# Hash attention and a quick-GELU feed-forward in fp32: the softmax divisors of a pair's two query halves in one TensorE step on four column quarters

## The chip, the cores and the metric

The kernel runs on one core of a Trainium2 chip. The metric is the device time of one launch in microseconds (us), as the median of several runs.

## What is computed

An attention block is followed by a feed-forward block, all in float32. Two positions may attend to each other only if the signs of six projections agree; a row sum of exponentials then divides each attention row.

```python
q_bits = (np.einsum('bhsd,dk->bhsk', q, proj) > 0).astype(np.int64)   # k_bits alike
mask = q_bucket[:, :, :, None] == k_bucket[:, :, None, :]
scores = np.where(mask, scale * np.matmul(q, k.transpose(0, 1, 3, 2)), -1000000000.0)
attn = np.exp(scores - np.max(scores, axis=-1, keepdims=True))
attn = attn / (np.sum(attn, axis=-1, keepdims=True) + 1e-09)
x = np.matmul(attn, v)                     # then (B, H, S, D) -> (B*S, H*D)
h = x @ w_in
g = h * (1.0 / (1.0 + np.exp(-1.702 * h)))
out = g @ w_out
```

B = 4, H = 8, S = 768, D = 64, so x is 3072 x 512; w_in is 512 x 2048 and w_out 2048 x 512, both handed over as 64-bit floats.

## The kernel before, in words

The heads are taken two at a time: 16 pairs, `pairs[n]`, with the two heads of a pair on partitions 0 to 63 and 64 to 127. The 768 queries of a pair are done in two halves of 384 columns (`HS`), c = 0 and c = 1. The loop at L525 runs over `groups`, which are these halves (those of pair 0 are each cut in two again), and hands out the work of group g together with what is left of the group before it, `prev`. The order of the instructions on TensorE (PE), VectorE (DVE), ScalarE (ACT) and GpSimd (POOL) is the order in which this Python code issues them (`manual_schedule`); the engines run side by side and wait for each other by semaphores. SyncE (SP) holds the DMA queue, in order too.

One group does the following.

- `scores` (L429): for each of six tiles of 128 keys, both heads, first a product of hash features in bf16 and then one of keys and queries in float32, into a PSUM tile `ps` (three buffers). ACT takes the exponential of each into `e` (L430); there is one `e` for c = 0 and one for c = 1.
- `add_low` on POOL (L437, L438) sums the exponentials of key tiles 0 to 2 into `acc0` (one buffer).
- `add_high` on DVE (L443, L445), for `prev`: sums key tiles 3 to 5 and `acc0` into `acc` (one buffer).
- `total` (L472), for `prev`: one matmul per head with a 128 x 64 block of ones. It sums `acc` over the 128 partitions and puts the sum on all 64 partitions of the head: `dn`, in PSUM, in a buffer that the hash products share (tag "m", one buffer).
- `invert` (L479, L481): DVE transposes `dn` in 32 x 32 blocks, so that of each block only one column is needed, and takes the reciprocals of 12 values per partition. In the next group `spread` (L486) transposes them back, broadcast over 32, and `norm` (L490) multiplies the attention output in `xT` by them.
- `values` (L453), for `prev`: the product of `e` and v into `av`; `unload` (L465, L466) on ACT takes it to `xT`.
- In a c = 0 group DVE turns k and q of the next pair (L388), ACT measures them (L395), and TensorE makes their hash products (`hashed`, L405); in the c = 1 group after it `featured` (L410) turns these into features on DVE, which DMAs (L417) spread to `kf` and `qf`.

In between, pairs 1 to 14 convert one chunk of w_in each from 64 to 32 bits (`convert`, L158). After the DMA into `raw` (L162) come six steps on DVE: L175, L179, L183, L190, L192, L195; with the third, ACT squares the high words into `size` (L187), which L195 reads. L575 issues `4 - c` steps per group: four in the c = 0 group, the last two in the c = 1 group. L579 then starts the next chunk's DMA, on SP's queue. In the last four pairs the c = 0 group also issues one of the sums `x_sums` (L577) for the feed-forward block.

After the pairs comes the feed-forward block: products L699 with w_in, the activation, products L812 with w_out, whose details the change does not touch. The last pair's second `total` is issued after the first part of it.

Of the kernel before, what the change touches and what calls it, by code (L numbers as in the profile page):

```python
# [8 lines left out]
F32 = mybir.dt.float32  # L9
BF16 = mybir.dt.bfloat16  # L10
I32 = mybir.dt.int32
U32 = mybir.dt.uint32
Act = mybir.ActivationFunctionType
Alu = mybir.AluOpType
# [5 lines left out]
P = 128  # L20
# [18 lines left out]
def kernel(  # L39
# [17 lines left out]
    nc = tc.nc  # L57

    loader = [nc.sync]
    B, H, S, D = q.shape  # L60
# [3 lines left out]
    T = S // P  # L64
# [3 lines left out]
    HS = HT * P  # L68
# [10 lines left out]
    ones = const.tile([P, D], F32, name="ones")  # L79
# [30 lines left out]
    for i, x in enumerate("kq"):  # L110
# [7 lines left out]
        for c in range(2):  # L118
            r0 = D * i + 32 * c
# [29 lines left out]
    CW = 512  # L149
# [3 lines left out]
    for x in (0x3FFFFFFF, 0xFF800000):  # L153
        m = const.tile([P, 1], U32, name=f"mask_{x:x}")
# [3 lines left out]
    def convert(cv, dst, src, queue=None, psum=None):  # L158


        raw = cv.tile([P, CW, 2], U32, tag="raw", name="raw")
        (queue or loader[0]).dma_start(out=raw, in_=src)  # L162

        def of(x):
            return x if len(dst.shape) == 2 else x.rearrange("p (x r) -> p x r", r=dst.shape[2])

        lo, hi = raw[:, :, 0], raw[:, :, 1]
        bits = cv.tile([P, CW], U32, tag="bits", name="bits")
        part = (cv if psum is None else psum).tile([P, CW], U32, tag="part", name="part")
        size = (cv if psum is None else psum).tile([P, CW], F32, tag="size", name="size")  # L170
        yield


        if psum is None:
            nc.vector.scalar_tensor_tensor(part, hi, 3, masks[0x3FFFFFFF], op0=Alu.logical_shift_left, op1=Alu.bitwise_and)  # L175
        else:
            nc.vector.tensor_scalar(part, hi, 3, 0x3FFFFFFF, op0=Alu.logical_shift_left, op1=Alu.bitwise_and)
        yield
        nc.vector.scalar_tensor_tensor(bits, hi, 0xC0000000, part, op0=Alu.bitwise_and, op1=Alu.bitwise_or)  # L179
        yield  # L180

        if psum is None:
            nc.vector.tensor_tensor(part, bits, masks[0xFF800000], op=Alu.bitwise_and)  # L183
        else:
            nc.vector.tensor_scalar(part, bits, 0xFF800000, None, op0=Alu.bitwise_and)

        nc.scalar.activation(size, hi.bitcast(F32), Act.Square)  # L187
        part = part.bitcast(F32)
        yield
        nc.vector.scalar_tensor_tensor(part, lo, 2.0**-52, part, op0=Alu.mult, op1=Alu.mult)  # L190
        yield
        nc.vector.tensor_tensor(dst, of(bits.bitcast(F32)), of(part), op=Alu.add)  # L192
        yield

        nc.vector.scalar_tensor_tensor(dst, of(size), (1.125 * 2.0**-15) ** 2, dst, op0=Alu.is_ge, op1=Alu.mult)  # L195
# [84 lines left out]
    def attention(ff):  # L280


        GT = T // 2
        actx = ExitStack()
        with actx:
            ld = actx.enter_context(tc.tile_pool(name="ld", bufs=1))
            wk = actx.enter_context(tc.tile_pool(name="wk", bufs=2))
            cv = actx.enter_context(tc.tile_pool(name="cv", bufs=1))
            st = actx.enter_context(tc.tile_pool(name="st", bufs=2))
            aps = actx.enter_context(tc.tile_pool(name="aps", bufs=1, space=PSUM))  # L290
            mps = actx.enter_context(tc.tile_pool(name="mps", bufs=1, space=PSUM))
# [140 lines left out]
            accs, avs = {}, {}  # L432
# [6 lines left out]

            def add_high(n, c):  # L440
                e = [es[c][:, GT + i, :, 0:HS] for i in range(GT)]
                acc = accs[n, c] = st.tile([P, 2, HS], F32, tag="acc", name="acc", bufs=1)
                nc.vector.scalar_tensor_tensor(acc, e[0], T * TINY, e[1], op0=Alu.add, op1=Alu.add)  # L443
                for x in (e[2], accs.pop((n, c, 0))):
                    nc.vector.tensor_tensor(acc, acc, x, op=Alu.add)  # L445
# [7 lines left out]
                        nc.tensor.matmul(av[D * j : D * (j + 1), :], vt[:, t, j, :], es[c][:, t, j, :],  # L453
                                         start=(t == 0), stop=(t == T - 1))

            def x_of(n, c):
                b, hp = pairs[n]
                x = xT[:, hp, b * S : (b + 1) * S]
                x = x.rearrange("d (t p) -> d t p", p=P) if n else x.rearrange("d (p t) -> d t p", p=P)
                return x[:, c * GT : (c + 1) * GT, :]  # L460

            def unload(n, c):
                av = avs.pop((n, c))
                vs = st.tile([P, 1], F32, tag="vs", name="vs")
                nc.scalar.copy(vs, av[:, HS : HS + 1])  # L465
                nc.scalar.activation(x_of(n, c), av[:, 0:HS].rearrange("p (t s) -> p t s", t=GT), Act.Identity, bias=vs[:, 0:1])  # L466

            def total(n, c):
                acc = accs.pop((n, c))
                dn = accs[n, c] = mps.tile([P, HS], F32, tag="m", name="dn")  # L470
                for j in range(2):
                    nc.tensor.matmul(dn[D * j : D * (j + 1), :], ones, acc[:, j, :], start=True, stop=True)  # L472

            def invert(n, c):


                dn = accs.pop((n, c))
                rt = st.tile([P, HS], F32, tag="rt", name="rt")
                nc.vector.transpose(rt, dn)  # L479
                r = st.tile([P, HS // 32, 1], F32, tag="r", name="r")  # L480
                nc.vector.reciprocal(r, rt.rearrange("p (s i) -> p s i", i=32)[:, :, 0:1])  # L481
                accs[n, c] = rt, r

            def spread(n, c):
                rt, r = accs[n, c]
                nc.vector.transpose(rt.rearrange("p (s i) -> p s i", i=32), r.to_broadcast([P, HS // 32, 32]))  # L486

            def norm(n, c):
                rt, r = accs.pop((n, c))
                nc.vector.tensor_tensor(x_of(n, c), x_of(n, c), rt.rearrange("p (t s) -> p t s", t=GT), op=Alu.mult)  # L490


            groups = [(n, c, kts) for n in range(len(pairs)) for c in range(2)
# [4 lines left out]
            def step(n, count=1):  # L498
                for _ in range(count):
                    next(conv.get(n, iter(())), None)  # L500
# [19 lines left out]
            totals, norms, hashes = [], [], []  # L520
# [4 lines left out]
            for g in range(len(groups) + 2):  # L525
                n, c, kts = groups[g] if g < len(groups) else (last + 1, 0, ())
                prev = groups[g - 1] if 1 <= g <= len(groups) else None
                if kts:
                    scores(n, c, kts)
                    if g == 0:  # L530
                        rest()
                    if kts[0] == 0:
                        add_low(n, c)


                if hashes:
                    featured(hashes.pop())
                ended = prev and prev[2][-1] == T - 1
                if ended:
                    add_high(*prev[:2])  # L540
                    totals.append((g + (g == len(groups) or len(kts) == GT), prev[:2]))
                for x in norms:
                    spread(*x)

                turned = ("", "k", "q", "")[g] if n == 0 else "kq" if c == 0 and n < last else ""
                for x in turned:
                    turn(n + 1, x)
                    measure(n + 1, x)
                if c == 1 or n == 0:
                    while norms:  # L550
                        norm(*norms.pop(0))
                inverted = []
                while totals and totals[0][0] == g:
                    inverted.append(totals.pop(0)[1])
                    total(*inverted[-1])
                    invert(*inverted[-1])
                while norms:
                    norm(*norms.pop(0))
                norms += inverted
                if prev:  # L560
                    values(*prev)
                if ended:
                    unload(*prev[:2])
                if "q" in turned:
                    hashed(n + 1)
                    if n:
                        hashes.append(n + 1)
                    else:
                        featured(n + 1)
                    for x in "kq":  # L570
                        if n + 2 <= last:
                            fetch(n + 2, x)
                    fetch_v(n + 1)
                if kts and kts[-1] == T - 1:
                    step(n, 4 - c)  # L575
                    if c == 0 and n > last - len(x_sums):
                        x_sums[n - last - 1]()  # L577
                    if c == 1:
                        begin(n + 1)  # L579
                if g == len(groups) - 1:  # L580
                    guard(0)
                if g == len(groups):
                    guard(1)
                    for f in in_sums(0):
                        f()
                    early.close()
                    next(ff)
            for x in norms:
                spread(*x)
                norm(*x)  # L590


    def shifted_attention():
# [405 lines left out]
```

## Time and profile before

| | us |
|---|---|
| median of 3 runs | 890.97 (890.84 to 891.78) |
| the profiled execution: its own time | 890.56 |
| its span, first to last instruction | 888.7 |
| attention, up to the first product of the feed-forward block | about 334 |
| one pair in the steady part of it | 20.04 |

How to read it. The span is what the profile sees of the profiled execution; the remaining 1.9 us of its own time lie outside of it. The page gives for each engine the busy time, then the chain of work that ended last: followed back from the last instruction, at each step to what released it. A timeline row has the start and the length in us, the engine, the line, the operation, what it writes and reads, and in brackets an idle time ahead of it with what ended it. `dn<-acc,ones` at L472 is `total`. A float32 matmul leaves two records in the trace: the 32 steps of `total`, two matmuls each, are 128 records.

The groups that the change touches, from the page and the answers on lines (mean ns of one):

| line | engine, what | count | mean ns |
|---|---|---|---|
| L472 | PE `dn<-acc,ones`, 128*64, 384 columns | 128 records | 512 |
| L405 | PE `hash<-kT,pf_k` and `hash<-qT,pf_q`, 128*32, 384 columns | 120 records | 498 |
| L479 | DVE transpose `rt<-dn` 128x384 | 32 | 580 |
| L481 | DVE reciprocal `r<-rt` 128x12 | 32 | 229 |
| L486 | DVE transpose `rt<-r` 128x384 | 32 | 572 |
| L490 | DVE product `xT<-xT,rt` 128x384 | 32 | 1020 (493 to 1816) |
| L187 | ACT square `size<-raw` 128x512 | 32 (16 of w_in) | 648 |
| L195 | DVE last conversion step, w_in 128x512 | 16 | 692 |

### The profile page before, as it was taken

Reading aid. Unit: us, or ns where it says so; the run is one execution under the profiler, and the core shown is the slowest. Engines: PE = TensorE matmul, PEld = TensorE weight load, DVE = VectorE, ACT = ScalarE, POOL = GpSimd, SP = SyncE. Lnnn points to the kernel's source line nnn. Section 1 sums busy time; section 2 is a strip of 40 time slices with the busy share of each in tenths; the row PEclk is TensorE's granted clock in tenths of the full one; section 3 lists DMA queues with packets and bytes.
Section 4 is the critical chain, followed back from the end, with each engine's and each line's share of the span. In section 5 each row is a group of like instructions: output and inputs, shape, how many; then the busy total and the mean of one; then the engine's idle time right before and its main releaser. Section 6 shows DMA issues by size and latency. Waiting matters only on the chain.

```text
span 888.7 us, 11969 instructions
## 1 busy us (share of the span) xinstructions
PE 873.2 (98%) x4077; PEld 503.5 (57%) x4077; DVE 709.3 (80%) x1020; ACT 313.9 (35%) x519; POOL 309.7 (35%) x275
## 2 busy tenths in 40 slices
PE   9899999999999999999999999999999999999995
PEld 4444444444444444444444444444888888888884
DVE  4698887888889964777788787888798977897785
ACT  5755666666665642233222223322100000000000
POOL 4243233222333263666434435559932000000000
PEclk9999999999999999999999999999999999999998
DMA  4745544556544103555455545565845665467524
GB/s 103 122 83 84 103 81 81 86 98 96 97 83 82 46 1 107 188 191 189 177 209 194 201 155 202 189 236 194 301 156 190 190 210 216 159 220 237 190 96 97
DMA packets 169477, 132.01 MB, mean 149 GB/s; under 512 B 123936, under 2 KB 138432, under 8 KB 164032
## 3 DMA queue, kind: packets, MB, share of 16 engines
q1 hardware_dynamic: 167712, 129.69, 51.0%
q10 hardware_dynamic: 1696, 1.48, 0.6%
q8 instruction: 34, 0.56, 0.3%
q14 instruction: 35, 0.29, 0.1%
HBM read 79.69 MB, written 50.33 MB: 146 GB/s over the span
## 4 chain that ended last, share of the span: by engine, by line
PE 96%; DVE 2%; DMA 1%; ACTq 0%; issue 0%; SPq 0%; ACT 0%; DVEq 0%
PE product L699 32%; PE product L812 28%; PE ps L429 16%; PE av L453 14%; PE dn L472 3%; PE hash L405 1%; DMA q<-in_q_dram 1%; PE tp L363 0%; ACTq L417 0%; DVE xT L816 0%; PE warm L356 0%; PE hash L370 0%; DVE y L791 0%; DVE acc L445 0%; SPq L325 0%
## 5 line engine op out<-in xcount | busy, mean ns | idle before, releaser
L430 ACT ACTIVATE e<-ps 128x768 f32<-128x768 f32 x192 | 151.5, 813 | 19.3 <-PE ps L429 13.4
L429 PE MATMUL ps<-qT,kT 64*128 64x384 f32 x768 | 155.1, 482 | 0.0
L699 PE MATMUL product<-xT,w_in_sb 128*128 128x512 f32 x288 | 135.4, 592 | 0.0
L453 PE MATMUL av<-e,v 128*64 128x385 f32 x768 | 130.2, 486 | 0.9 <-ACT xT L466 0.9
L437 POOL TENSOR_TENSOR acc<-e 128x768 f32<-128x768 f32 x32 | 49.6, 1551 | 208.1 <-ACT e L430 103.3
L707 ACT ACTIVATE c<-c 128x512 f32<-128x512 f32 x72 | 45.5, 632 | 186.2 <-issue 78.8
L453 PEld LDWEIGHTS av<-e,v 128*64 128x64 f32 x768 | 54.9, 136 | 70.5 <-issue 69.0
L699 PEld LDWEIGHTS product<-xT,w_in_sb 128*128 128x128 f32 x288 | 54.6, 190 | 68.5 <-issue 63.4
L699 PE MATMUL product<-t_x,s_in 128*128 128x512 f32 x192 | 90.2, 592 | 0.0
L429 PEld LDWEIGHTS ps<-qT,kT 64*128 64x128 f32 x768 | 68.2, 188 | 35.5 <-issue 35.5
L216 POOL TENSOR_TENSOR v<-c,u 128x512 f32<-128x512 f32 x24 | 34.3, 1427 | 129.2 <-ACT c L707 129.2
L818 ACT COPY u<-product 128x256 f32<-128x256 f32 x21 | 7.8, 373 | 167.7 <-PE product L812 125.6
L429 PE MATMUL ps<-qf,kf 64*128 64x384 bf16 x384 | 63.0, 324 | 0.7 <-ACT e L430 0.5
L699 PEld LDWEIGHTS product<-t_x,s_in 128*128 128x128 f32 x192 | 36.5, 190 | 45.9 <-issue 43.8
L438 POOL TENSOR_TENSOR acc<-acc,e 128x768 f32<-128x768 f32 x32 | 56.7, 1772 | 2.5
L699 PE MATMUL product<-xT,s_in 128*128 128x512 f32 x96 | 45.1, 592 | 0.0
L699 PE MATMUL product<-t_x,w_in_sb 128*128 128x512 f32 x96 | 45.1, 592 | 0.0
L429 PEld LDWEIGHTS <-kf 64*128 64x128 bf16 x384 | 18.9, 94 | 42.2 <-issue 20.7
L479 DVE STREAM_TRANSPOSE rt<-dn 128x384 f32<-128x384 f32 x32 | 18.6, 580 | 25.7 <-PE dn L472 25.6
L465 ACT COPY vs<-av 128x1 f32<-128x1 f32 x32 | 5.1, 160 | 95.0 <-PE av L453 94.9
L812 PE MATMUL product<-raw_g,xT 128*128 128x256 f32 x152 | 35.1, 379 | 0.0
L490 DVE TENSOR_TENSOR xT<-xT,rt 128x384 f32<-128x384 f32 x32 | 32.6, 1020 | 1.7
(201 smaller groups left out, 1558.3 us busy)
## 6 DMA issues: line engine op xcount, KB each, us to landing
raw_g<-g_dram SPq DMA_DIRECT2D x22, 1024.0 KB
s_in<-g_dram SPq DMA_DIRECT2D x20, 1024.0 KB
g_dram<-c SPq DMA_DIRECT2D x72, 256.0 KB
g_dram<-t SPq DMA_DIRECT2D x48, 256.0 KB
raw<-in_moe_w_out_dram SPq DMA_DIRECT2D x16, 512.0 KB
raw<-in_moe_w_in_dram SPq DMA_DIRECT2D x15, 512.0 KB
v<-in_v_dram SPq DMA_DIRECT2D x32, 192.0 KB
g_dram<-u SPq DMA_DIRECT2D x24, 256.0 KB
```

The source lines that it names most:

```text
L216: return [lambda: eng.tensor_tensor(t1, b12, b11, op=Alu.subtract), lambda: eng.tensor_tensor(b12, b22, b12, op=Alu.subtract), lambda: eng ...
L429: nc.tensor.matmul(ps[:, j, 0:HS], a[hs, keys], m[hs, cols], start=not last, stop=last)
L430: nc.scalar.activation(es[c][:, kt, :, 0:HS], ps[:, :, 0:HS], Act.Exp, scale=1.0 / D**0.5)
L437: nc.gpsimd.tensor_tensor(acc, es[c][:, 0, :, 0:HS], es[c][:, 1, :, 0:HS], op=Alu.add)
L438: nc.gpsimd.tensor_tensor(acc, acc, es[c][:, 2, :, 0:HS], op=Alu.add)
L453: nc.tensor.matmul(av[D * j : D * (j + 1), :], vt[:, t, j, :], es[c][:, t, j, :], start=(t == 0), stop=(t == T - 1))
L472: nc.tensor.matmul(dn[D * j : D * (j + 1), :], ones, acc[:, j, :], start=True, stop=True)
L479: nc.vector.transpose(rt, dn)
L490: nc.vector.tensor_tensor(x_of(n, c), x_of(n, c), rt.rearrange("p (t s) -> p t s", t=GT), op=Alu.mult)
L699: nc.tensor.matmul(ps, wq[LEFT[i]][:, kc, :], xq[RIGHT[i]][:, kc, :], start=(kc == 0), stop=(kc == K2 - 1))
L707: nc.scalar.activation(c, c, Act.Gelu_apprx_sigmoid)
L812: nc.tensor.matmul(ps, wq[LEFT[i]][:, c, :], gq[RIGHT[i]][:, c, :], start=(c == 0), stop=(c == F4 - 1))
```

## The change

`total` now runs once per pair, after the sums of both halves are there: four matmuls with a 128 x 32 block of ones, each onto 32 partitions of `dn` (head j, half c on partitions 64 j + 32 c). `acc` has two buffers for it. `invert` transposes `dn` once; a reciprocal of 24 values per partition (the 12 values twice) fills `r`, and four small reciprocals, one for each strip of 32 partitions, put in what belongs to the other half: they read one strip and write another. One transpose of 768 columns spreads them, in the same group. `norm` multiplies 768 columns at once, in the group after. `rt` and the spread `rs` have one buffer each.

The conversion of w_in gives up the tiles `part` and `size`: `part` is made in the destination, and the square overwrites the high words in `raw`. `step` gets `2 + 2 * c`: two steps in the c = 0 group, four in the c = 1 group. In the order of the built program the changed instructions stand so: in a c = 0 group DVE has the sums of the c = 1 half before, turned k and q, `rt`, five reciprocals, the spread, two conversion steps; in a c = 1 group the features, the sums, the norm, four conversion steps. On ACT the square stands behind the unload of the c = 1 group, ahead of the exponentials of the next pair.

```diff
-        part = (cv if psum is None else psum).tile([P, CW], U32, tag="part", name="part")
-        size = (cv if psum is None else psum).tile([P, CW], F32, tag="size", name="size")
+        if psum is None:
+            part, size = dst.bitcast(U32), hi.bitcast(F32)
+        else:
+            part = psum.tile([P, CW], U32, tag="part", name="part")
+            size = psum.tile([P, CW], F32, tag="size", name="size")
...
-                acc = accs[n, c] = st.tile([P, 2, HS], F32, tag="acc", name="acc", bufs=1)
+                acc = accs[n, c] = st.tile([P, 2, HS], F32, tag="acc", name="acc")
...
-            def total(n, c):
-                acc = accs.pop((n, c))
-                dn = accs[n, c] = mps.tile([P, HS], F32, tag="m", name="dn")
-                for j in range(2):
-                    nc.tensor.matmul(dn[D * j : D * (j + 1), :], ones, acc[:, j, :], start=True, stop=True)
+            def total(n):
+                dn = accs[n] = mps.tile([P, HS], F32, tag="m", name="dn")
+                for c in range(2):
+                    acc = accs.pop((n, c))
+                    for j in range(2):
+                        r0 = D * j + 32 * c
+                        nc.tensor.matmul(dn[r0 : r0 + 32, :], ones[:, 0:32], acc[:, j, :], start=True, stop=True)
...
+            def invert(n):
+                dn = accs.pop(n)
+                rt = st.tile([P, HS // 32, 32], F32, tag="rt", name="rt", bufs=1)
+                nc.vector.transpose(rt.rearrange("p s i -> p (s i)"), dn)
+                r = st.tile([P, 2, HS // 32], F32, tag="r", name="r")
+                nc.vector.reciprocal(r, rt[:, :, 0].unsqueeze(1).to_broadcast([P, 2, HS // 32]))
+                for r0 in range(0, P, 32):
+                    c = r0 // 32 % 2
+                    r1 = r0 + 32 - 64 * c
+                    nc.vector.reciprocal(r[r1 : r1 + 32, c], rt[r0 : r0 + 32, :, 0])
+                rs = accs[n] = st.tile([P, S], F32, tag="rs", name="rs", bufs=1)
+                nc.vector.transpose(rs.rearrange("p (s i) -> p s i", i=32),
+                                    r.rearrange("p c s -> p (c s)").unsqueeze(2).to_broadcast([P, S // 32, 32]))
+
+            def norm(n):
+                x, rs = x_of(n), accs.pop(n)
+                nc.vector.tensor_tensor(x, x, rs.rearrange("p (t s) -> p t s", t=T), op=Alu.mult)
...
-                    totals.append((g + (g == len(groups) or len(kts) == GT), prev[:2]))
-                for x in norms:
-                    spread(*x)
+                    if prev[1] == 1:
+                        totals.append((g + (g == len(groups)), prev[0]))
...
                 while norms:
-                    norm(*norms.pop(0))
-                norms += inverted
+                    norm(norms.pop(0))
+                if totals and totals[0][0] == g:
+                    norms.append(totals.pop(0)[1])
+                    total(norms[-1])
+                    invert(norms[-1])
...
-                    step(n, 4 - c)
+                    step(n, 2 + 2 * c)
```

More of the change, by code (lines that the diff above doesn't have):

```diff
@@ L454, in values, with x_of @@
                                          start=(t == 0), stop=(t == T - 1))
-            def x_of(n, c):
+            def x_of(n):
                 b, hp = pairs[n]
                 x = xT[:, hp, b * S : (b + 1) * S]
-                x = x.rearrange("d (t p) -> d t p", p=P) if n else x.rearrange("d (p t) -> d t p", p=P)
-                return x[:, c * GT : (c + 1) * GT, :]
+                return x.rearrange("d (t p) -> d t p", p=P) if n else x.rearrange("d (p t) -> d t p", p=P)
             def unload(n, c):
@@ L465, in unload @@
                 nc.scalar.copy(vs, av[:, HS : HS + 1])
-                nc.scalar.activation(x_of(n, c), av[:, 0:HS].rearrange("p (t s) -> p t s", t=GT), Act.Identity, bias=vs[:, 0:1])
-            def total(n, c):
-                acc = accs.pop((n, c))
-                dn = accs[n, c] = mps.tile([P, HS], F32, tag="m", name="dn")
-                for j in range(2):
[L472 to L490, printed above, removed]
+                nc.scalar.activation(x_of(n)[:, c * GT : (c + 1) * GT, :], av[:, 0:HS].rearrange("p (t s) -> p t s", t=GT), Act.Identity, bias=vs[:, 0:1])
@@ L548, in attention @@
                     measure(n + 1, x)
-                if c == 1 or n == 0:
-                    while norms:
-                        norm(*norms.pop(0))
[L552 to L556, printed above, removed]
-                while norms:
-                    norm(*norms.pop(0))
-                norms += inverted
+                while norms:
+                    norm(norms.pop(0))
[3 more added lines that the diff above has]
+                    invert(norms[-1])
                 if prev:
@@ L588, in attention @@
             for x in norms:
-                spread(*x)
-                norm(*x)
+                norm(x)
     def shifted_attention():
```

## The prediction, made before the changed kernel was run

> **What bounds the kernel now.** I read the busy shares, then the chain that ended last in order of time, then each engine's timeline over one steady pair of heads.
>
> ```profile
> PE 873.2 (98%) x4077; PEld 503.5 (57%) x4077; DVE 709.3 (80%) x1020; ACT 313.9 (35%) x519; POOL 309.7 (35%) x275
> ```
>
> TensorE is nearly always busy. The chain over one steady pair (start us, us, what):
>
> ```profile
> 199.07 0.78 PE hash L405 x8
> 199.85 4.95 PE ps L429 x36
> 204.81 0.80 PE dn L472 x4
> 205.60 3.88 PE av L453 x24
> 209.48 4.95 PE ps L429 x36
> 214.44 0.80 PE dn L472 x4
> 215.23 3.88 PE av L453 x24
> ```
>
> The chain is TensorE alone, without gaps: 2 x (4.95 + 0.80 + 3.88) + 0.78 = 20.04 us per pair. Each step (half of the queries) pays 0.80 for `dn`. The hash, whose four outputs are 32 partitions each, does 8 records in 0.78; `dn` does 4 in 0.80.
>
> The timelines say what stands behind it (start us, us, engine, line):
>
> ```profile
> 207.88 0.69 DVE L195 SCALAR_TENSOR_TENSOR w_in_sb<-size,w_in_sb 128x512 f32<-128x512 f32 x1
> 208.50 0.95 DVE L443 SCALAR_TENSOR_TENSOR acc<-e 128x768 f32<-128x768 f32 x1
> 209.55 0.96 DVE L445 TENSOR_TENSOR acc<-acc,e 128x768 f32<-128x768 f32 x1
> 210.61 0.96 DVE L445 TENSOR_TENSOR acc<-acc,acc 128x768 f32<-128x768 f32 x1
> ...
> 215.28 0.58 DVE L479 STREAM_TRANSPOSE rt<-dn 128x384 f32<-128x384 f32 x1 [1.50 <-PE dn L472]
> ...
> 219.35 0.58 ACT L466 ACTIVATE xT<-av,vs 128x384 f32<-128x384 f32 x1
> 219.83 0.66 ACT L187 ACTIVATE size<-raw 128x512 f32<-128x512 f32 x1
> ...
> 224.23 1.51 DVE L490 TENSOR_TENSOR xT<-xT,rt 128x384 f32<-128x384 f32 x1
> 236.09 0.50 DVE L490 TENSOR_TENSOR xT<-xT,rt 128x384 f32<-128x384 f32 x1
> ```
>
> The sums `acc` are complete at 211.57, while TensorE asks for them only at 214.37: 2.8 us of slack. DVE is busy 17.10 us of 20.05 (stage table), so it is the next engine in line.
>
> **What the Trainium skill says.** "TensorE: Matmul & The Clock Gate", Part 3 on packing: matmuls whose outputs lie in different strips of 32 partitions run side by side. The hash agrees: four starts within 0.02 us (219.04 to 219.06). "TensorEngine Tiling (Array Packing)", Key Properties: a change of tiling mode drains TensorE. No cost shows: `av` takes 3.88 before a hash and before scores alike. "SBUF — State Buffer", Who interferes with whom: a VectorE instruction with two SBUF inputs and a GpSimd instruction exclude each other. The trace agrees: L490 took 1.51 while L437 ran on POOL, 0.50 without. "VectorE: DVE Perf Modes", Two Vector instructions with no wait between them: an instruction that starts in another quadrant than the one before is held until that has finished; this concerns the four small reciprocals, and no row of before shows it.
>
> **The change, part by part** (t counts from the start of a pair's first scores, 209.42 in these timelines).
>
> *TensorE.* Before 32 x 0.80 = 25.6 us; after, 16 steps of four quarters at the hash's 0.78 = 12.5. Bounds for the new step: 0.78, or 1.6 if quarters ran two by two; the hash has the same 128x32 weights and 384 columns, so I take 0.78. That is 0.82 per pair, 13.1 gross.
>
> *Start.* Pairs 0 and 1 don't get it. Without pair 0's first `dn` (25.68) the next scores still wait until 29.03, for ACT, which issues DMAs from 24.05 to 27.9. Without pair 1's first `dn` (44.39, 1.51 idle before it) TensorE runs ahead to 46.7, but the DVE is behind: it starts at 35.58, when q has landed, and has qT 0.98, rt 0.54, reciprocals 1.3, spread 0.9, two conversion steps 1.3, f 0.6, three sums 3.1, norm 1.0, three conversion steps 2.0 and some 2 to 3 us of POOL's lock ahead of L198 (L195 before), then 3.1 of sums: about 53.7, so pair 1's `dn` is at about 53.7 against 54.02. I take a gain of 0.3 (0 to 0.9). There remain 14 x 0.82 = 11.5.
>
> *The conversion's place.* Four, then two steps become two, then four; and `size` now lies in `raw`. On ACT the square L190 (L187 before) thus stands behind the second step's unload, just ahead of the next pair's exponentials; on DVE the last conversion step waits for it and stands ahead of L446/L448, the sums that the joint `dn` needs. This is the added wait. From the rows: vs at t = 0.11, unload at 0.30, square 0.48 later at 0.78, done at 1.44 (0.66); conversion step at 1.49, the next instruction 0.62 later at 2.11; the three sums as before 1.05 + 1.06 + 0.96, done at 5.18; TensorE at 5.23. It asks at 4.95. So 0.28; I take 0.30 (0 to 0.6). The first half's two matmuls do not wait and fill part of it. It affects the pairs 3 to 15 that follow a conversion, 13 x 0.30 = 3.9. The exponentials start about 0.38 later (1.46 for 1.10). The fourth scores tile, at 2.42, needs the first at 2.3: covered by 0.1; uncovered it costs that excess per pair.
>
> *DVE's chain.* Does it reach that step before the square has? From 1.49: step 0.62, sums 3.0, turns 1.72, rt 0.62; one reciprocal of 24 elements (12 take 0.23; 0.23 to 0.46, I take 0.33) and four of 12 (held: 0.23 each, range 0.14 to 0.45) with two waits 1.35; spread at the price of L388 0.94, next after 0.87; two conversion steps 1.32: t = 10.95. Hash's feature 0.60, sums 3.0, norm 0.96 (as L445; before two of 0.50 to 1.51): 15.5. Then three conversion steps with two SBUF inputs, 1.9 us, against POOL's pair 1.54 + 1.68, which starts when the sums free `acc0`: all serial, 20.8. The square is done at 19.5 + 1.44 = 21.0, the period being 20.04 - 0.80 - 0.02 + 0.30 = 19.5. So DVE is in time by 0.2 us: thin. In pairs 12 to 14 the x sums (issued at L577; 1.22 each, row L218) make it late by 0.9 at most, less where DVE takes the lock first; I take 0.5, 3 x 0.5 = 1.5.
>
> *Edits costed at nothing.* The unload is unchanged. Writing `part` into the destination moves no work. `raw` is free only when the last step has ended (t = 2.1), so its DMA, issued at -1.2 before, goes at about 2.2; the next issues behind it on SP wait for turned k anyway (216.15, t = 6.7). The DMA activity of before ends some 3 us after its issue, so it lands near 5.5, needed at 9.6: cover 4 us, and beyond it each us is on DVE's chain. The feature DMAs follow the k, q and v fetches on SP as before; the scores that need them come 0.8 earlier, and the four that the first tile needs were issued 3.8 us before it. The last pair's `dn` lies in the feed-forward stage in both. The square's strided write is unshown; I take 0.66, double would add 0.6 to each stall.
>
> *Sum.* 11.5 + 0.3 - 3.9 - 1.5 = 6.4 us. The profiled execution took 890.56 (span 888.7): 884.2. The median of the runs is 0.41 above it: 890.97 - 6.4 = **884.6**.
>
> **Rivals.** *B, no stall*: the square or the sums come a little earlier than summed, or TensorE's queue covers 0.28. For: 0.28 is small beside my roundings. Against: every term is a row. 11.5 + 0.9 gained: 878.6. *C, DVE binds without losing all*: small reciprocals near 0.35 or a worse order of the lock bring its chain to about 19.9. For: 0.2 us of cover. Gain 10 x 0.14 + 0.3, less 3 x (1.1 - 0.14) for the x sums: about -1, 892 at worst, 889 where the x sums find room; I set 890.3. *D, slower*: the same engine past the old period. Place: the serial stretch of reciprocals, spread and conversion ahead of the sums. It decides where the chain passes 20.04, 0.8 above my sum, as with held reciprocals of 0.45 together with a lock lost once more per pair: at 20.4, 13 x 0.36 + 3 x 1.1 - 0.3 = 7.7 lost, 898.7. Against: DVE does less in sum (two transposes of 0.58, two spreads of 0.57, two norms before). *E, the quarters don't run side by side*: `dn` stays at 1.6 per pair, and the wait lies under its first half; no gain, 890.9. Against: the hash.
>
> **Chances.** A, the forecast, 0.54 (own range 882 to 887.5); B 0.17; C 0.15; D 0.10; E 0.04. A measurement can tell about 0.2%, 1.8 us, from no change: 889.2 to 892.8 is the same. Faster: A, B and a third of C, 0.76; the same: E and the rest of C, 0.14; slower: D, 0.10. The range 879 to 890 takes in A, most of B and the better half of C.
>
> **What would show it.** Right: 16 groups of `dn`, 128x32, each about 0.78 in the chain; one period near 19.5; a short TensorE idle (about 0.3) ahead of `dn` released by the sums; DVE idle before the last conversion step, released by the square. B: no idle there, period 19.2. C and D: no DVE idle anywhere in the pair, TensorE idle before `dn` of 0.7 or more. Wrong altogether: `dn` near 1.6, or DVE waiting for `raw`.

## The result and the profile after

| | before | changed |
|---|---|---|
| median, six runs of each | 891.15 us | 887.89 us (886.93 to 889.4) |
| profiled execution: own time, span | 890.56, 888.7 | 887.43, 885.6 |

The ratio is 0.9965, with a 95% interval of 0.9952 to 0.9977: 3.3 us faster, where 6.4 were forecast. The time lies in the stated range of 879 to 890, but just above the forecast's own 882 to 887.5, and the gain is half of the forecast. The page after begins:

```profile
PE 869.4 (98%) x4077; PEld 501.0 (57%) x4077; DVE 723.3 (82%) x1020; ACT 309.2 (35%) x519; POOL 320.7 (36%) x275
```

TensorE still sets the time. The chain of the changed kernel over one steady pair (start us, us, what):

```profile
212.53 0.96 PE dn L477 x8
213.50 4.03 PE av L456 x24
217.53 0.78 PE hash L408 x8
218.31 4.95 PE ps L432 x36
223.26 4.03 PE av L456 x24
227.30 4.95 PE ps L432 x36
232.25 0.96 PE dn L477 x8
```

A pair now takes 232.25 - 212.53 = 19.72 us for 20.04 before. One `dn` of 0.80 is gone. The other one is eight records and takes 0.96, and both `av` take 4.03 where they took 3.88. This last difference was in no step of the prediction.

The wait that the change added, around one pair's end: VectorE first, then ScalarE. L190 is the square, L198 the last conversion step, L446 and L448 the sums.

```profile
203.12 2.03 DVE L186 TENSOR_TENSOR w_in_sb<-bits,mask_ff 128x512 uint32<-128x512 uint32 x1
205.19 2.05 DVE L193 SCALAR_TENSOR_TENSOR w_in_sb<-raw,w_in_sb 128x512 f32<-128x512 uint32 x1
207.27 0.69 DVE L195 TENSOR_TENSOR w_in_sb<-bits,w_in_sb 128x512 f32<-128x512 f32 x1
208.99 0.69 DVE L198 SCALAR_TENSOR_TENSOR w_in_sb<-raw,w_in_sb 128x512 f32<-128x512 f32 x1 [1.02 <-ACT raw L190]
...
211.65 0.96 DVE L448 TENSOR_TENSOR acc<-acc,acc 128x768 f32<-128x768 f32 x1
```

```profile
207.82 0.58 ACT L468 ACTIVATE xT<-av,vs 128x384 f32<-128x384 f32 x1
208.30 0.66 ACT L190 ACTIVATE raw<-raw 128x512 f32<-128x512 f32 x1
```

The last conversion step waits 1.02 us for the square, which ends at 208.96. The sums follow it and end at 212.61. The scores of this pair began at 207.52 in the timeline, so that is t = 5.09 where the prediction said 5.18, against a TensorE that asks at 4.95.

Where the 3.1 us of the two profiled spans came from, by landmarks of the two chains:

| stretch | before | changed | gain |
|---|---|---|---|
| start to pair 1's hash (22.44, 23.39) | 22.44 | 23.39 | -0.95 |
| to pair 3's hash (58.77, 59.78) | 36.33 | 36.39 | -0.06 |
| twelve pairs, to pair 15's hash (299.29, 296.73) | 240.52 | 236.95 | 3.57 |
| to `row`, the end of attention (333.94, 330.57) | 34.65 | 33.84 | 0.81 |
| feed-forward, to the end of the span | 554.76 | 555.03 | -0.27 |

The attention from the first hash on gained 4.32 us. The first stretch is the same code in both; in the profiles of the six kernels below it ended between 23.16 and 24.38, so the 22.44 of the kernel before is a quick start of that one execution and not an effect of the change.

### The profile page after: what moved, and what is told of

Its sections match the earlier page's. It is cut to its first block, busy times and chain, and to the rows that moved or that the text cites. A ratio compares the mean times of both kernels' runs of the same rounds, so it can differ in the third digit from the quotient of the medians.

```text
span 885.6 us, 11940 instructions
## 1 busy us (share of the span) xinstructions
PE 869.4 (98%) x4077; PEld 501.0 (57%) x4077; DVE 723.3 (82%) x1020; ACT 309.2 (35%) x519; POOL 320.7 (36%) x275
## 4 chain that ended last, share of the span: by engine, by line
PE 96%; DVE 2%; ACTq 0%; ACT 0%; issue 0%; DVEq 0%
PE product L699 33%; PE product L812 28%; PE ps L432 17%; PE av L456 14%; PE dn L477 2%; PE hash L408 1%; PE tp L366 1%; DVE acc L448 0%; ACTq L420 0%; DVE xT L816 0%; PE warm L359 0%; PE hash L373 0%; DVE y L791 0%; DVE w_in_sb L193 0%; DVE w_in_sb L186 0%
## 5 line engine op out<-in xcount | busy, mean ns | idle before, releaser
L433 ACT ACTIVATE e<-ps 128x768 f32<-128x768 f32 x192 | 148.4, 811 | 23.5 <-PE ps L432 18.3
L440 POOL TENSOR_TENSOR acc<-e 128x768 f32<-128x768 f32 x32 | 58.7, 1833 | 195.4 <-DVE acc L448 185.9
L456 PEld LDWEIGHTS av<-e,v 128*64 128x64 f32 x768 | 52.1, 136 | 77.6 <-issue 75.5
L441 POOL TENSOR_TENSOR acc<-acc,e 128x768 f32<-128x768 f32 x32 | 59.1, 1847 | 2.5
L446 DVE SCALAR_TENSOR_TENSOR acc<-e 128x768 f32<-128x768 f32 x32 | 30.5, 953 | 7.7 <-ACT e L433 7.7
L448 DVE TENSOR_TENSOR acc<-acc,e 128x768 f32<-128x768 f32 x32 | 32.0, 999 | 2.4
```

Of the source, the lines that this page charges most:

```text
L433: nc.scalar.activation(es[c][:, kt, :, 0:HS], ps[:, :, 0:HS], Act.Exp, scale=1.0 / D**0.5)
L440: nc.gpsimd.tensor_tensor(acc, es[c][:, 0, :, 0:HS], es[c][:, 1, :, 0:HS], op=Alu.add)
L441: nc.gpsimd.tensor_tensor(acc, acc, es[c][:, 2, :, 0:HS], op=Alu.add)
```

## The experiments

The *tiling* of a group of matmuls is what the trace's rows give as `64*128`, `128*64` or `128*32`: the shape of the block of weights that one of its float32 matmuls uses. Here the scores are 64x128, the values 128x64, the hash 128x32; the total was 128x64 before and is 128x32 now. Each experiment compares with the kernel before, run again beside it.

Theory 1, made from the two chains: a group of matmuls that follows one of another tiling pays an *entry* of about 0.15 us. The 0.80 of the old `dn` contained this entry. With `dn` gone, `av` stands behind the scores and pays it; and the new `dn`, on quarters, makes `av` pay it in the other step too. It can be seen in the weight loads (PEld). In the kernel before, after the 128x64 `dn`:

```profile
204.73 0.20 PEld L472 LDWEIGHTS dn<-acc,ones 128*64 128x64 f32 x4 [0.55 <-issue]
205.11 0.14 PEld L453 LDWEIGHTS av<-e,v 128*64 128x64 f32 x2 [0.18 <-issue]
```

`av` starts at 205.43 there: its first weights are loaded 0.32 us ahead, beside `dn`. In the changed kernel, after the 128x32 `dn`:

```profile
212.46 0.34 PEld L477 LDWEIGHTS dn<-acc,ones 128*32 128x32 f32 x8 [0.55 <-issue]
213.43 0.20 PEld L456 LDWEIGHTS av<-e,v 128*64 128x64 f32 x4 [0.62 <-issue]
```

`av` starts at 213.43, with its first load: nothing is loaded ahead. The rival, theory 2: `av` is slower for a reason of its own, or four quarters cost by their number of records.

**Only the tiling.** The kernel before, with each total on quarters:

```diff
-                    nc.tensor.matmul(dn[D * j : D * (j + 1), :], ones, acc[:, j, :], start=True, stop=True)
+                    for r0 in (D * j, D * j + 32):
+                        nc.tensor.matmul(dn[r0 : r0 + 32, :], ones[:, 0:32], acc[:, j, :], start=True, stop=True)
```

> The kernel before, with each of its 32 totals written as four 128x32 matmuls (each head's sum onto its two strips of 32 partitions) instead of two 128x64; same sums, everything else alike. Theory 1 (a change of TensorE's column tiling costs about 0.10 at the gap and 0.05 at the first step of the group that follows, because the weights can't be loaded ahead): dn and av are now in different tilings, so 0.15 more per total, a pair takes 20.34 instead of 20.04, about 4.8 us more in all: 896. Theory 2 (av is slower in the changed kernel for another reason, such as what its values or its buffer wait for; four quarters cost no more than two halves): a pair stays at 20.04, 891.

Measured: 896.78 us for 891.31 of the kernel before, ratio 1.006 (95% interval 1.0043 to 1.0076). Its chain:

```profile
203.75 4.95 PE ps L429 x36
208.70 0.78 PE dn L473 x8
209.48 4.03 PE av L453 x24
```

`dn` itself is no slower, 0.78. `av` goes from 3.88 to 4.03 although nothing about it was edited; a pair takes 20.32. Theory 1's price holds, and theory 2's first half falls. From pair 3's hash to `row` the profiled execution took 3.7 us more than before; most of the rest of the 5.5 lies ahead of pair 3's hash (at 60.75 for 58.77) and is not assigned.

**Only the number of instructions.** Each total as four 128x64 matmuls of 192 columns:

```diff
-                    nc.tensor.matmul(dn[D * j : D * (j + 1), :], ones, acc[:, j, :], start=True, stop=True)
+                    for x in (slice(0, HS // 2), slice(HS // 2, HS)):
+                        nc.tensor.matmul(dn[D * j : D * (j + 1), x], ones, acc[:, j, x], start=True, stop=True)
```

> The kernel before, with each total written as four 128x64 matmuls of 192 columns instead of two of 384: twice the instructions and weight loads, as in the four-quarter form, but no change of tiling between dn and av. Theory 1 (the change of tiling costs): no more than the two extra weight loads at most hidden, a pair within 0.05 of 20.04, 891 to 892. Rival (the number of matmul and weight-load records is what costs in the four-quarter form): 0.15 more per total as in the kernel with quarters, 896.

Measured: 892.73 us, ratio 1.0015 (1.0006 to 1.0024). Its chain:

```profile
206.89 0.81 PE dn L473 x8
207.69 3.88 PE av L453 x24
```

Eight records, one tiling: `av` stays at 3.88 and `dn` grows by 0.01. Theory 2's second half falls too: it is the tiling that costs, not the count. The pairs add some 0.4 us of the 1.4; the rest lies ahead of pair 3's hash here too (60.68 for 58.77) and stays unassigned.

**The square one group earlier.** The changed kernel with three steps in each group. The third step on VectorE, L186, goes to the earlier group together with the square:

```diff
-                    step(n, 2 + 2 * c)
+                    step(n, 3)
```

> The changed kernel with the conversion's steps dealt three and three, so that the square on ScalarE stands in the c = 0 group and no DVE step waits for it ahead of the sums. Theory 1 (the 0.17 of idle inside dn is the wait for the square, passed on through the sums): dn falls from 0.96 to 0.79, a pair from 19.71 to 19.54, 13 x 0.17 + 0.5 = 2.7 us less: 885.2. Rival (VectorE's amount of work before the sums, its turns, reciprocals and POOL's lock, sets the sums' end): dn stays near 0.96 or grows, 887.9 or more.

Measured: 885.24 us, ratio to before 0.9929 (0.9912 to 0.9946). Its chain:

```profile
206.00 4.95 PE ps L432 x36
210.96 0.78 PE dn L477 x8
211.74 4.03 PE av L456 x24
```

`dn` is back at 0.78 and a pair takes 19.53, as forecast. The run alone can't tell the square's wait from one conversion step less on VectorE ahead of the sums. The rows above can: in the changed kernel VectorE stood idle for 1.02 before L198, so less work would have brought the sums no earlier. The wait for the square was all of the difference between 0.96 and 0.78 in these pairs; pairs 13 and 14, with their x sums, still show 0.96 and 1.21. The joint step without the wait is worth 20.04 - 19.53 = 0.51 per pair, not 0.82.

**The total beside a group of its own tiling.** The changed kernel, with the order of TensorE in a c = 0 group now scores, values, total, hash. From pair 2 on the hash is put into a scores buffer, since `dn` ahead of it holds the shared one, and the inversion goes to the c = 1 group:

```diff
-                h = dots[n] = mps.tile([P, HS], F32, tag="m", name="hash")
+                h = dots[n] = mps.tile([P, HS], F32, tag="m", name="hash") if n < 2 else sps.tile([P, 2, 512], F32, tag="s", name="hash")[:, 0, 0:HS]
...
                 while norms:
+                    invert(norms[0])
                     norm(norms.pop(0))
+                if prev:
+                    values(*prev)
                 if totals and totals[0][0] == g:
                     norms.append(totals.pop(0)[1])
                     total(norms[-1])
-                    invert(norms[-1])
-                if prev:
-                    values(*prev)
...
```

> The changed kernel with the joint total moved behind the values, directly ahead of the next pair's hash products, which have the same 128x32 tiling; the hash takes a scores buffer instead of the shared one, and the inversion goes to the c = 1 group, ahead of the norm. Theory 1: one change of tiling per pair goes (scores, av, dn, hash, scores instead of scores, dn, av, hash, scores): 0.15 less, and the sums have 4 us more, so the 0.17 of waiting goes too: a pair at 19.39 instead of 19.71, 14 x 0.32 + 0.5 = 5.0 us less than the changed kernel: 883. Theory 2 (the loss is av's own, or the change of tiling is free): only the wait goes, 19.54, 885.2. If the third scores tile waits for the hash's buffer, it is slower than either.

Measured: 879.87 us, ratio 0.9868 (0.9851 to 0.9884). Its chain:

```profile
207.84 4.03 PE av L456 x24
211.87 0.78 PE dn L477 x8
212.66 0.65 PE hash L408 x8
```

The hash, whose matmuls are the same, falls from 0.78 to 0.65: `dn` ahead of it has paid the entry. A pair takes 19.40, for 19.39 by theory 1. That the hash's new buffer did it is a rival which the last run below takes up. The time is 3 us better than expected, most of it at the start: from pair 1's hash to pair 3's it takes 57.48 - 23.59 = 33.89 for 36.33 before. TensorE asks for pair 1's sums only after the values, 4 us later, and VectorE has them 1.9 us sooner than in the changed kernel (29.5 us after pair 1's hash, for 31.5), because L186 and L193 do not meet POOL's sums there (0.67 and 0.69, for 2.02 and 2.06).

**What one total gives back.** The kernel before, with the c = 0 totals, inversions and norms left out, so that half of the attention output stays undivided:

```diff
-                    totals.append((g + (g == len(groups) or len(kts) == GT), prev[:2]))
+                    if prev[1] == 1:
+                        totals.append((g + (g == len(groups) or len(kts) == GT), prev[:2]))
```

> The kernel before with the total, inversion and norm of the c = 0 halves left out (half of the attention output stays undivided): what one dn gives back by itself, with no square ahead of the sums and no change of tiling between dn and av. Theory 1 (the chain's 0.80 for dn contains the entry into its tiling, which av then has to pay): a pair falls by 0.65 to 19.39, 15 to 16 times: about 10 us, 881. The prediction's price (0.80 all goes): a pair at 19.24, about 12.6 us, 878.7.

Measured: 880.21 us, ratio 0.988 (0.9863 to 0.9896). Its chain:

```profile
198.51 4.04 PE av L453 x24
202.54 4.95 PE ps L429 x36
207.49 0.80 PE dn L472 x4
208.29 3.88 PE av L453 x24
```

Both cases side by side in one kernel: behind the scores `av` takes 4.04, behind a `dn` of its own tiling 3.88. Removing 0.80 from the chain returned 20.04 - 19.40 = 0.64 per pair. The time fell by 0.9 us more than expected; here too the start was shorter (pair 3's hash at 56.98, 33.78 after pair 1's).

**All of it in one tiling.** On top of the kernel beside the hash, the values on quarters as well:

```diff
-                        nc.tensor.matmul(av[D * j : D * (j + 1), :], vt[:, t, j, :], es[c][:, t, j, :],
-                                         start=(t == 0), stop=(t == T - 1))
+                        for h in range(2):
+                            r0 = D * j + 32 * h
+                            nc.tensor.matmul(av[r0 : r0 + 32, :], vt[:, t, j, 32 * h : 32 * (h + 1)], es[c][:, t, j, :],
+                                             start=(t == 0), stop=(t == T - 1))
```

> The kernel with the joint total beside the hash, with the values' matmuls also written as 128x32 quarters (each head's 64 columns as two strips): av, dn and hash of a c = 0 group are then of one tiling. Theory 1: dn falls from 0.78 to 0.65, av stays at 4.03 where four quarters stream as fast as two halves; a pair at 19.26 instead of 19.40, 16 x 0.14 = 2.2 us less than the kernel beside the hash, 877.7. Rival: twice as many weight loads and matmuls (96 records each per group) don't go through in the same time, av grows by some tenths of a us, and it is slower than the kernel beside the hash.

Measured: 878.15 us, ratio 0.9853 (0.9837 to 0.987), the fastest kernel here. Its chain:

```profile
207.15 4.02 PE av L458 x48
211.17 0.65 PE dn L479 x8
211.82 0.65 PE hash L408 x8
```

Twice the records in the same time, and `dn` is at 0.65 too: both groups behind `av` come without an entry. A pair takes 19.23; the time is 0.4 us above the expected one.

This also settles what the hash's buffer did. Pair 1's hash keeps the old buffer in both kernels and stands directly behind `av`. Its row in the kernel of the total beside the hash (values on halves), then in this one (values on quarters):

```profile
23.59 0.83 PE hash L408 x8
```

```profile
24.38 0.69 PE hash L408 x8
```

With the tiling of `av` alone changed, it falls by 0.14.

**One sum for all of them.** Take 4.95 for each scores group, 3.88 for each `av`, 0.65 for each `dn` and hash, and add 0.15 for each change into 128x64 and 0.13 for each into 128x32; these figures are read from the rows above, so this only shows that the rows agree. It gives 20.04 us for a pair of the kernel before, 19.52 for the changed kernel without its wait of 0.18, and 20.30, 20.04, 19.52, 19.39, 19.39 and 19.22 for the six runs in order; measured were 20.04, 19.72 with the wait, and 20.32, 20.07, 19.53, 19.40, 19.40 and 19.23. The merge took away one total, but a pair now changes tiling six times where it changed five times.

## Why the prediction was off: its steps one by one

**TensorE, 0.82 per pair: the step that failed.** The prediction priced the removed total at 0.80, its row in the chain. It had cited the drain at a change of tiling and dismissed it with "No cost shows: `av` takes 3.88 before a hash and before scores alike". That looked at the group ahead of a change; the cost is booked on the group behind it, in `dn`'s 0.80 and the hash's 0.78. A total streams for 0.65 (`dn` in the last run) and the entry is 0.13 to 0.15. So removing one gave 0.65, since `av` then pays the entry behind the scores, and the quarters cost `av` another 0.15 in the step that keeps a total: 0.80 + 0.02 - 0.15 - 0.15 = 0.52 by the rows, and 0.51 by the run with steps three and three. Over 14 pairs this is 14 x (0.82 - 0.51) = 4.3 us too much.

The warning was in the timeline: `dn` starts at 204.74 and `av` at 205.43, 0.69 apart, not 0.80.

**Start, 0.3 gained.** The mechanism was right and the gain was nil: from pair 1's hash to the end of its joint `dn` 0.08 gained, then 0.15 lost by `av`'s entry (-0.06 up to pair 3's hash). TensorE ran ahead and then waited 1.54 us inside pair 1's `dn` for VectorE:

```profile
52.53 0.84 PE L477 MATMUL dn<-acc,ones 128*32 128x384 f32 x4
54.91 0.84 PE L477 MATMUL dn<-acc,ones 128*32 128x384 f32 x4 [1.54 <-DVE acc L448]
```

The first four records, of the half whose sums were ready, did go ahead.

**The wait for the square, 13 x 0.30.** The mechanism was right, in place, cause and order; the size was 0.96 - 0.78 = 0.18, shown by dealing the steps three and three.

**VectorE's chain, in time by 0.2 us; the x sums, 3 x 0.5.** It was in time by 1.02: ready at t = 20.16 for the summed 20.8, with the square done at 21.16 for 21.0. The terms as listed add up to 20.6, not 20.8. Two of the conversion steps met POOL's sums and took 2.03 and 2.05 instead of 0.69, which is the lock that the prediction counted; the rest of the difference no run here assigns. In the pairs with an x sum L198 no longer waited for the square, VectorE itself was late, and `dn` took up to 1.14:

```profile
271.68 1.12 PE dn L477 x8
...
291.56 1.14 PE dn L477 x8
```

That is 0.16 to 0.18 more than 0.96, for 0.5: right in kind, too large in size.

**Edits costed at nothing** held: the square's strided write took 0.66, no first conversion step waited for `raw`, and in the steady part every scores group took 4.95, as before.

**The sum again** with what was measured: 14 x 0.51 - 0.06 - 10 x 0.18 - 3 x 0.35 = 4.2, against 4.32 in the two traces from the first hash to the end of attention. The rest between that and the 3.3 of the medians is the start of the launch and 0.27 in the feed-forward block, whose code is the same; no run here assigns it.

So the step that failed was 4.3 us too high, while the waits, put at 3.9 + 1.5 = 5.4, cost 2.85. That the forecast gain missed by only 3.1 us is partly luck: the second error took 2.5 us off the first.

Of the rivals, B (no stall) fell with the row of 1.02 and the run three and three. C and D (VectorE binds) fell with VectorE's idle time. E (quarters one after another) fell with the 0.78. None of them was what took the gain.

Whether the entry is a drain or only the weights that are not loaded ahead is not settled: wherever an entry was paid, the loads were late too, and no run separates the two.

## What to carry to other kernels

A group's row in a chain can hold the cost of entering it. Before pricing its removal, ask which group will stand behind the same predecessor and whether that one then pays; where the next group has the same tiling, the distance from its start to the start of that group, and the group's first weight load, tell. (Where the next group has another tiling, the distance does not: a `dn` of quarters ahead of `av` shows 0.78 either way.) Where small matmul groups of different tilings alternate, put those of one tiling next to each other, or bring them to one tiling, before merging them: here the merged total was worth 3.3 us where it was put, 11.4 beside the hash, and 13.0 with the values on quarters too. Not all of that is tiling: moving the total also took away the waits inside `dn`, for the square and in the pairs with x sums, and some 2.5 us at the start.

## What the runs showed of the hardware that was not expected

- A change of TensorE's tiling, from 64x128 to 128x64, from 128x64 to 128x32 or from 128x32 back to 128x64, cost the group behind it 0.13 to 0.15 us in the kernels here. What a change back to 64x128 costs is not shown: the scores took 4.95 behind every other group, and no run puts them behind their own tiling.
- The first weights of a group behind a change were loaded as it started (`av` at 213.43); behind a group of its own tiling they were loaded ahead, by 0.32 us behind matmuls of 384 columns and by 0.17 behind those of 192.
- 128x32 quarters kept up with 128x64 halves in float32 also over a long group: 48 records in 4.02 us for 24 in 4.03.
- A reciprocal of 24 values per partition took 0.30 us where one of 12 took 0.23; four of 12 values on 32 partitions, each from another strip, took 0.92 together, one after another.
